# Score visits of four heads in one four-bank PSUM tile, and segment 0 cut into two query halves

## The chip, the core and the metric

The kernel runs on one core of a Trainium2 chip. A core has a matrix engine (PE, TensorE), a vector engine (DVE), an activation engine (ACT), a general engine (POOL, GpSimd), a sequencer that issues most DMAs (SP), an on-chip memory of 128 partitions (SBUF), and eight accumulation banks (PSUM) of 512 fp32 columns per partition, into which the matmuls of this kernel write. Each engine has a queue of its own instructions, in the order in which the program was compiled, and waits for others through semaphores. A matmul here is a weight load and a moving operand that is streamed past the weights; its moving columns are given in the text.

The metric is the device time of one execution in microseconds (us): the median of several runs.

## The reference

One transformer block on x of 2048 rows and 576 columns in bf16: attention with a compressive memory, then an FFN. Cut to what matters (32 heads of 18 columns, four segments of 512 rows; `phi(t)` is `t+1` above zero and `exp(t)` below):

```
h  = x + attention(layernorm(x)) @ wo
for s in range(4):                     # 512 rows each
    p     = softmax(qs @ ks.T * scale + causal mask)
    a_dot = p @ vs
    a_mem = (phi(qs) @ M) / (phi(qs) @ z + 1e-6)
    o     = g * a_mem + (1 - g) * a_dot          # g = sigmoid(beta), per head
    M, z  = M + phi(ks).T @ vs, z + sum(phi(ks))
h2 = h + gelu(layernorm(h) @ w1 + b1) @ w2 + b2  # inner width 4608
```

## The kernel before

**Phases.** The rows are 16 tiles of 128, four per segment. The program text calls `phase_P`, `phase_A`, `phase_B` for segments 0 to 3, and after them `phase_C` four times. Nobody writes the engines' orders by hand: a scheduler lays each engine's instructions in order by program order, priority and its own notion of when operands are ready. So the FFN's matmuls (phase C, last in the text) are put wherever PE would otherwise wait, and once compiled the order of each engine's queue is fixed. In what follows they are called filler.

- P (L218): per tile a layernorm (statistics on DVE, a power on POOL L182, scaling L183), five transposes (L195), a copy (ACT), 30 matmuls with 288 moving columns for Q, K and V (L203, L205), copies into padded layouts (ACT L72, DVE L268), 16 transposes (L259, L264) and their copies into `QT_al_s`, `KT_al_s` (DVE L260, L265). wq, wk and wv are loaded again for each segment through `load_w` (L102). At its end the memory matrix is updated (32 matmuls, L281).
- A (L300): eight groups of four heads. A group has three steps of key tiles: tile 0 (512 query columns), tiles 1 and 3 (384 and 128), tile 2 (256). In a step four heads' score matmuls use 32 rows of the PE array each (L338). They go into two tiles of two banks (`unit2`, L186; two buffers), two heads in each; each tile is followed by its own exponential (L347). POOL masks each diagonal block (L349), and PE multiplies the result with V (L356, 40 matmuls of 19 columns per group) into `ox`, which has one buffer. From segment 1 on each group has the memory part too: an exponential (L312), POOL L314, DVE L316, four matmuls (L323), normalising (L326 to L328). DVE ends the group at L361 to L371.
- B (L378): per tile five transposes, copy, ten matmuls with wo (all into one `unit2`), the residual add (L392), layernorm, five transposes, copy into `xn2T_s`. The two transpose results share a second `unit2`, one bank each.
- C (L405): per segment 36 blocks of FFN1 (five matmuls of 512 columns, L419 and L420, into one of three `psC` banks, DVE copy L424), a gelu after each twelve blocks (ACT L428, in place), and FFN2: per tile two chains of 36 matmuls of 288 columns (L437).

PSUM is split 2x2 banks (`psS`), 1 (`psX`), 3 (`psC`).

Of the kernel before, what the change touches and what calls it, by code (L numbers as in the profile page):

```python
# [8 lines left out]
ACT = mybir.ActivationFunctionType  # L9
# [7 lines left out]
def kernel(  # L17
# [15 lines left out]
    dbg = None  # L33
    nseg_run = None
# [15 lines left out]
    XW = 640  # L50
    scale = float(Dh) ** -0.5
    EPS = 1e-5
    BIG = 3.0e38
    GB = 3
    FORCE4 = False
    HIPRI = True
    GB = 3
    EVAC_ACT = 0
    XT_DVE = False
    QK_DVE = False  # L60

    def copy_xt(out, in_):
        if XT_DVE:
            nc.vector.tensor_copy(out=out, in_=in_)
        else:
            nc.scalar.copy(out=out, in_=in_)  # L66

    def copy_qk(out, in_):
        if QK_DVE:
            nc.vector.tensor_copy(out=out, in_=in_)  # L70
        else:
            nc.scalar.copy(out=out, in_=in_)  # L72
    if nseg_run is None:
        nseg_run = NSEG
# [3 lines left out]
    wpool = ctx.enter_context(tc.tile_pool(name="wpool", bufs=1))  # L78
# [5 lines left out]
    ptpool = ctx.enter_context(tc.tile_pool(name="ptpool", bufs=2))  # L84
    ptpool1 = ctx.enter_context(tc.tile_pool(name="ptpool1", bufs=1))
    hpool = ctx.enter_context(tc.tile_pool(name="hpool", bufs=2))
    hbpool = ctx.enter_context(tc.tile_pool(name="hbpool", bufs=1))
# [3 lines left out]
    psS = ctx.enter_context(tc.tile_pool(name="psS", bufs=2, space=PSUM))  # L91
    psX = ctx.enter_context(tc.tile_pool(name="psX", bufs=1, space=PSUM))
    psC = ctx.enter_context(tc.tile_pool(name="psC", bufs=3, space=PSUM))

    x_pre = []
    for tl in range(TPS):
        xt = xpool.tile([P, D], BF16, tag="x", name="xt") if tl < 2 else None
        if xt is not None:
            nc.sync.dma_start(out=xt[:], in_=x[tl * P:(tl + 1) * P, :])
        x_pre.append(xt)  # L100

    def load_w(W, tag):  # L102
        wt = wpool.tile([P, KT, D], BF16, tag=tag, name="wt_" + tag)
        nc.sync.dma_start(out=wt[:, 0:4, :], in_=W[0:512, :].rearrange("(k p) n -> p k n", p=P))
        nc.sync.dma_start(out=wt[0:64, 4, :], in_=W[512:576, :])
        nc.gpsimd.memset(wt[64:KTAIL, 4, :], 0.0)
        return wt

    w_pre = {"wq": load_w(A_wq, "wq"), "wk": load_w(A_wk, "wk"), "wvo": load_w(A_wv, "wvo")}
# [3 lines left out]
    maskcol = const.tile([P, 1], F32, name="maskcol")  # L113
    nc.vector.memset(maskcol[:], 0.0)
    for i in range(4):
        nc.vector.memset(maskcol[32 * i:32 * i + Dh, :], 1.0)
# [3 lines left out]
    beta_bc = const.tile([P, H], BF16, name="beta_bc")  # L120
    nc.sync.dma_start(out=beta_bc[:], in_=A_beta.partition_broadcast(P))
    g_bc = const.tile([P, H], F32, name="g_bc")
    nc.scalar.activation(out=g_bc[:], in_=beta_bc[:], func=ACT.Sigmoid)
    omg_bc = const.tile([P, H], F32, name="omg_bc")
    nc.vector.tensor_scalar(out=omg_bc[:], in0=g_bc[:], scalar1=-1.0, scalar2=1.0, op0=ALU.mult, op1=ALU.add)
    gmzm = const.tile([P, G, Dh], F32, name="gmzm")
    for i in range(4):
        src = g_bc[32 * i:32 * i + 32, :].rearrange("p (g i) -> p g i", i=4)[:, :, i:i + 1]
        nc.vector.tensor_scalar(out=gmzm[32 * i:32 * i + 32, :, :], in0=src.to_broadcast([32, G, Dh]),
                                scalar1=maskcol[32 * i:32 * i + 32, :], scalar2=None, op0=ALU.mult)  # L130

    b2_bc = const.tile([P, D], BF16, name="b2_bc")
    nc.sync.dma_start(out=b2_bc[:], in_=B_b2.partition_broadcast(P))
    b1_row = B_b1.rearrange("(o f) -> o f", o=1)
# [6 lines left out]
    q_pads = [const.tile([P, H, 32], BF16, name=f"q_pad{j}") for j in range(2)]  # L141
    k_pads = [const.tile([P, H, 32], BF16, name=f"k_pad{j}") for j in range(2)]
    phik_pads = [const.tile([P, H, 32], BF16, name=f"phik_pad{j}") for j in range(TPS)]
    v_augs = [const.tile([P, H, Dh + 1], BF16, name=f"v_aug{j}") for j in range(TPS)]
    xn_bufs = [const.tile([P, XW], BF16, name=f"xn{j}") for j in range(2)]
    xn2_bufs = [const.tile([P, XW], BF16, name=f"xn2_{j}") for j in range(1)]
    o_nat = const.tile([P, TPS, XW], BF16, name="o_nat")
    for tx in xn_bufs:
        nc.gpsimd.memset(tx[:, D:XW], 0.0)
    for tpad in q_pads + k_pads:  # L150
        nc.gpsimd.memset(tpad[:, :, Dh:32], 0.0)
    for tpad in phik_pads:
        nc.vector.memset(tpad[:, :, Dh:32], 0.0)
    for tv in v_augs:
        nc.vector.memset(tv[:, :, Dh:Dh + 1], 1.0)
    for tx in xn2_bufs:
        nc.gpsimd.memset(tx[:, D:XW], 0.0)
        nc.gpsimd.memset(tx[:, D:D + 1], 1.0)
    nc.gpsimd.memset(o_nat[:, :, D:XW], 0.0)

    hd = tc.dram_tile([S, D], F32, name="hd")
# [3 lines left out]
    late = {"x_last": None, "w2_last": None}  # L165

    def issue_w2():
        for c in range(4):
            d = nc.sync.dma_start(out=w2_sb[:, c * 9:(c + 1) * 9, :], in_=w2v[:, c * 9:(c + 1) * 9, :])
            if late["x_last"] is not None:  # L170
                tc.add_manual_dep(d.ins, late["x_last"].ins.name, SYNC_DEP, reason="bulk FFN weights after the first segment's inputs")
            late["w2_last"] = d
# [13 lines left out]
    def unit2():  # L186
        return psS.tile([P, 2, 512], F32, tag="st2", name="u2")

    def bf16v(bank_ap):
        return bank_ap.bitcast(BF16)  # L190

    def transposes5(src, bank_ap):
        pt = bf16v(bank_ap)[:, 0:KT * P].rearrange("p (k q) -> p k q", q=P)
        for k in range(KT):
            nc.tensor.transpose(out=pt[:, k, :], in_=src[:, k * P:(k + 1) * P], identity=ident[:])  # L195
        return pt

    def proj(xT_t, wt):
        u = unit2()
        for hf in range(2):  # L200
            ps = u[:, hf, :]
            for k in range(4):
                nc.tensor.matmul(out=ps[:, 0:HALF], lhsT=xT_t[:, k, :], rhs=wt[:, k, hf * HALF:(hf + 1) * HALF],  # L203
                                 start=(k == 0), stop=False)
            nc.tensor.matmul(out=ps[:, 0:HALF], lhsT=xT_t[0:KTAIL, 4, :], rhs=wt[0:KTAIL, 4, hf * HALF:(hf + 1) * HALF],  # L205
                             start=False, stop=True)
        return u

    def hview(u):
        return u[:, :, 0:HALF].rearrange("p b (h d) -> p b h d", d=Dh)  # L210

    def pad_view(tpad):
        return tpad[:, :, 0:Dh].rearrange("p (b h) d -> p b h d", b=2)

    st_P = {}
    st_B = {}

    def phase_P(s):  # L218
        if s == 0:
            wq_t, wk_t, wv_t = w_pre["wq"], w_pre["wk"], w_pre["wvo"]  # L220
        else:
            wq_t = load_w(A_wq, "wq")
            wk_t = load_w(A_wk, "wk")
            wv_t = load_w(A_wv, "wvo")
        QT_al_s = alpool.tile([P, G, L], BF16, tag="qt", name="QT_al_s")
        KT_al_s = alpool.tile([P, G, L], BF16, tag="kt", name="KT_al_s")
        for tl in range(TPS):
            t = s * TPS + tl
            cols = slice(tl * P, (tl + 1) * P)
            if s == 0 and x_pre[tl] is not None:  # L230
                xt = x_pre[tl]
            else:
                xt = xpool.tile([P, D], BF16, tag="x", name="xt")
                xd = nc.sync.dma_start(out=xt[:], in_=x[t * P:(t + 1) * P, :])
                if s == 0:
                    late["x_last"] = xd
                    if tl == TPS - 1:
                        issue_w2()
            xn = xn_bufs[tl % 2]
            layernorm(xt[:], xn)  # L240
            u0 = unit2()
            pt = transposes5(xn, u0[:, 0, :])
            xnT_t = xtp.tile([P, KT, P], BF16, tag="xnT", name="xnT_t")
            copy_xt(xnT_t[:], pt)
            uq = proj(xnT_t, wq_t)
            q_pad = q_pads[tl % 2]
            copy_qk(pad_view(q_pad), hview(uq))
            if dbg is not None and "q" in dbg:
                nc.sync.dma_start(out=dbg["q"][t * P:(t + 1) * P, :].rearrange("p (h d) -> p h d", d=Dh), in_=q_pad[:, :, 0:Dh])
            uk = proj(xnT_t, wk_t)  # L250
            k_pad = k_pads[tl % 2]
            copy_qk(pad_view(k_pad), hview(uk))
            ek = tmp1.tile([P, H, Dh], BF16, tag="e", name="ek")
            nc.scalar.activation(out=ek[:].rearrange("p (b h) d -> p b h d", b=2), in_=hview(uk), func=ACT.Exp)
            ut = unit2()
            ptq = bf16v(ut[:, 0, :]).rearrange("p (g q) -> p g q", q=P)
# [188 lines left out]
    if mode == "attn_first":  # L445
# [4 lines left out]
        for s in range(n):  # L450
            phase_C(s)
# [46 lines left out]
```

## Time and profile before

| what | value |
|---|---|
| three runs | 618.3, 619.83 (median), 621.29 us |
| span of the profiled execution | 618.1 us |
| mean granted PE clock | 0.939 |
| busy: PE, DVE, ACT, POOL | 553.5, 327.6, 319.4, 154.1 us |
| DMA | 54.65 MB, 88 GB/s in the mean |
| longest wait groups | POOL L401 for DVE L392 76.2 us; ACT L428 for DVE L424 55.7 us |

The page of a profile gives the busy time of each engine and, in 40 slices of 15.5 us, how busy each was and which clock PE was granted. A view by windows gives the same sums for chosen stretches: for each engine its busy time and, in brackets, its instructions. A view by time lists instructions: start, duration, engine, line, operation, output and inputs, sizes, count, and in square brackets the idle time before it with what ended it. A duration is not a price: FFN2's matmuls last 286 ns each by their rows, but 36 of them in a row take 4.41 us, 122.5 ns each. The distance from one start to the next is what a matmul costs PE. Idle time of an engine that sets nothing costs nothing.

### The profile page before, as it was taken

To read this page: it belongs to the slowest core of one execution; us is meant where nothing else is said; L and a number is where in the kernel's file an instruction comes from. 1 tells how busy PE (TensorE), PEld (TensorE's weight loads), DVE (VectorE), ACT (ScalarE), POOL (GpSimd) and SP (SyncE) were. 2 spreads that over 40 slices of the span, in tenths; PEclk is the share of its full clock that TensorE was granted. 3 is DMA by queue.
4 is the path that set the end of the run, shared out by engine and by line. 5 is a ranking of instruction groups with operands and counts; after the bars stand their busy time and mean duration, and the time that the engine had idled before them with its cause. 6 is when DMAs were issued, how large, how long until landed. Compare 5 with 4: busy or idle time off the path is not lost. (4 is left out here: it accounts for less than half of the span.)

```text
span 618.1 us, 12146 instructions
## 1 busy us (share of the span) xinstructions
PE 553.5 (90%) x4992; PEld 331.1 (54%) x4992; DVE 327.6 (53%) x811; ACT 319.4 (52%) x342; POOL 154.1 (25%) x247
## 2 busy tenths in 40 slices
PE   2778875599999998999999998899999999999997
PEld 1553333375444566675444466665544567744576
DVE  5443223467777635647786735555687641166310
ACT  1449951134999931338788742368767540024300
POOL 3124432313342223224323123135331210000000
PEclk9995555599999999999999999999999999999999
DMA  7960003325223113322132333111124432144020
GB/s 194 351 201 3 2 1 97 110 65 147 65 79 110 45 59 123 104 75 85 43 89 67 114 117 117 58 45 30 31 78 116 109 123 77 38 135 129 25 58 20
DMA packets 48223, 54.65 MB, mean 88 GB/s; under 512 B 3204, under 2 KB 44072, under 8 KB 48168
## 3 DMA queue, kind: packets, MB, share of 16 engines
q1 hardware_dynamic: 48168, 53.88, 29.3%
q8 instruction: 39, 0.64, 0.4%
q14 instruction: 16, 0.13, 0.1%
HBM read 46.79 MB, written 7.08 MB: 87 GB/s over the span
## 5 line engine op out<-in xcount | busy, mean ns | idle before, releaser
L437 PEld LDWEIGHTS <-hT 128*128 128x128 bf16 x1152 | 107.5, 98 | 30.3 <-issue 3.5
L428 ACT ACTIVATE hT<-hT 128x6144 bf16<-128x6144 bf16 x12 | 63.9, 5324 | 55.8 <-DVE hT L424 55.7
L419 PEld LDWEIGHTS <-w1g 128*128 128x128 bf16 x576 | 51.3, 98 | 56.0 <-issue 7.4
L203 PEld LDWEIGHTS <-xnT_t 128*128 128x128 bf16 x384 | 36.7, 100 | 24.3 <-ACT xnT_t L66 13.4
L338 PEld LDWEIGHTS <-KT_al_s 32*128 32x128 bf16 x512 | 21.0, 93 | 50.9 <-issue 47.9
L401 POOL TENSOR_TENSOR hb<-h_t,b_bc 128x576 f32<-128x576 f32 x16 | 20.4, 1277 | 76.2 <-DVE h_t L392 76.2
L182 POOL TENSOR_TENSOR rstd<-rstd,mhalf 128x1 f32<-128x1 f32 x32 | 17.5, 549 | 40.3 <-DVE rstd L181 40.3
L314 POOL TENSOR_SCALAR r_g<-QT_al_s 128x512 bf16<-128x512 bf16 x24 | 14.7, 612 | 36.1 <-DVE pq L316 33.4
L420 PEld LDWEIGHTS <-w1g 65*128 65x128 bf16 x144 | 14.0, 97 | 14.4 <-issue 0.6
L312 ACT ACTIVATE e_g<-QT_al_s 128x512 bf16<-128x512 bf16 x24 | 15.1, 630 | 11.4 <-DVE pq L316 8.0
L203 PEld LDWEIGHTS <-oT_t 128*128 128x128 bf16 x128 | 13.6, 109 | 11.0 <-issue 4.2
L316 DVE SCALAR_TENSOR_TENSOR pq<-e_g,r_g 128x512 bf16<-128x512 bf16 x24 | 19.2, 801 | 0.3
L195 PEld LDWEIGHTS <-xn_0_167 128*128 128x128 bf16 x80 | 5.2, 107 | 22.5 <-DVE xn_0_167 L183 21.6
L308 DVE MEMSET ox<- 128x456 f32 x32 | 14.0, 438 | 3.6 <-DVE o_nat L365 1.4
L177 DVE BATCH_NORM_STATS2 stats<-xt 128x6 f32<-128x288 bf16 x32 | 13.5, 441 | 3.9 <-DMA xt<-in_A_x_dram 3.8
L183 DVE TENSOR_SCALAR xn_0_167<-h_t,mv,rstd 128x576 bf16<-128x576 f32 x16 | 9.3, 579 | 9.9 <-POOL rstd L182 9.9
L323 PEld LDWEIGHTS <-pq 128*128 128x128 bf16 x96 | 8.1, 97 | 11.9 <-issue 5.6
L177 DVE BATCH_NORM_STATS2 stats<-h_t 128x6 f32<-128x288 f32 x32 | 13.1, 451 | 0.4
L270 POOL TENSOR_SCALAR rk<-k_pad_155 128x576 bf16<-128x576 bf16 x8 | 5.4, 678 | 28.0 <-ACT k_pad_155 L72 28.0
L205 PEld LDWEIGHTS <-xnT_t 65*128 65x128 bf16 x96 | 9.7, 101 | 2.8
L270 POOL TENSOR_SCALAR rk<-k_pad_156 128x576 bf16<-128x576 bf16 x8 | 5.3, 666 | 21.9 <-ACT k_pad_156 L72 21.2
L428 ACT ACT_TABLE_LOAD x8 | 10.3, 1283 | 0.1
(1911 smaller groups left out, 1416.8 us busy)
## 6 DMA issues: line engine op xcount, KB each, us to landing
w1g<-in_B_w_dram SPq DMA_DIRECT2D x36, 512.0 KB
w_sb<-in_B_w_dram SPq DMA_DIRECT2D x4, 1296.0 KB
hd<-hb SPq DMA_DIRECT2D x16, 288.0 KB
hc<-hd SPq DMA_DIRECT2D x16, 288.0 KB
xt<-in_A_x_dram SPq DMA_DIRECT2D x16, 144.0 KB
wt_wq<-in_A_wq_dram SPq DMA_DIRECT2D x4, 576.0 KB
wt_wk<-in_A_wk_dram SPq DMA_DIRECT2D x4, 576.0 KB
wt_wvo<-in_A_wv_dram SPq DMA_DIRECT2D x4, 576.0 KB
```

Of the source, the lines that this page charges most:

```text
L177: nc.vector.bn_stats(out=stats[:, c, :], in_=src[:, c * HALF:(c + 1) * HALF])
L182: nc.gpsimd.tensor_tensor(out=rstd[:], in0=rstd[:], in1=mhalf[:], op=ALU.pow)
L203: nc.tensor.matmul(out=ps[:, 0:HALF], lhsT=xT_t[:, k, :], rhs=wt[:, k, hf * HALF:(hf + 1) * HALF], start=(k == 0), stop=False)
L308: nc.vector.memset(ox[:, 0:456], 0.0)
L312: nc.scalar.activation(out=e_g[:], in_=QT_al_s[:, g, :], func=ACT.Exp)
L314: nc.gpsimd.tensor_scalar(out=r_g[:], in0=QT_al_s[:, g, :], scalar1=BIG, scalar2=0.0, op0=ALU.min, op1=ALU.max)
L316: nc.vector.scalar_tensor_tensor(out=pq[:], in0=e_g[:], scalar=1.0, in1=r_g[:], op0=ALU.min, op1=ALU.add)
L338: mm = nc.tensor.matmul(out=sts[i // 2][:, i % 2, off:off + n], lhsT=KT_al_s[rows, g, kt * P:(kt + 1) * P], rhs=QT_al_s[rows, g, kt * P:L] ...
L401: nc.gpsimd.tensor_tensor(out=hb[:], in0=h_t[:], in1=b2_bc[:], op=ALU.add)
L419: nc.tensor.matmul(out=ps[:], lhsT=w1g[:, k, j * P:(j + 1) * P], rhs=xn2T_s[:, k, :], start=(k == 0), stop=False)
L428: nc.scalar.activation(out=hT[:, f0:f1, :], in_=hT[:, f0:f1, :], func=ACT.Gelu_apprx_tanh)
L437: nc.tensor.matmul(out=ps[:, 0:HALF], lhsT=hT[:, f, tl * P:(tl + 1) * P], rhs=w2_sb[:, f, hf * HALF:(hf + 1) * HALF], start=(f == 0), stop ...
```

## The change

1. **Score visits.** PSUM is split 4 (`psS`, one buffer of four banks), 1 (`psX`), 2 (`psC`), 1 (`psB`). A "visit" puts the scores of four heads, one per bank, for up to 512 columns of (group, key tile) pairs into the one `banks4()` tile, followed by one exponential over all four banks. Written-out plans (`VISITS`) pack pairs of neighbouring groups into full visits: 20 per segment.
2. **One bank for the rest.** Transposes, the wo product (in two halves), the memory product and the memory update each take the single `bank()` (`psB`). FFN banks go from three to two.
3. **Projection.** wq, wk and wv lie side by side in a resident tile, loaded once; Q, K and V of a tile are four chains of five matmuls with 432 columns. wo is resident too. The mask on `KT_al_s` is dropped.
4. **Segment 0 in halves.** P, A and B run for tiles 0 and 1, and then for tiles 2 and 3; the FFN of each half is a unit of its own, whose FFN1 matmuls have 256 moving columns. w1 is so streamed five times and not four.
5. **Memory part.** All four query tiles in one product, with no clearing of the output between them.
6. **Start.** beta is loaded on POOL's queue, wk on ACT's; the gate is computed with an exponential and a reciprocal, after the first two tiles' projection. w2 comes in six DMAs after the inputs of segment 0's second half.

```diff
-    psS = ctx.enter_context(tc.tile_pool(name="psS", bufs=2, space=PSUM))
+    psS = ctx.enter_context(tc.tile_pool(name="psS", bufs=1, space=PSUM))
     psX = ctx.enter_context(tc.tile_pool(name="psX", bufs=1, space=PSUM))
-    psC = ctx.enter_context(tc.tile_pool(name="psC", bufs=3, space=PSUM))
+    psC = ctx.enter_context(tc.tile_pool(name="psC", bufs=2, space=PSUM))
+    psB = ctx.enter_context(tc.tile_pool(name="psB", bufs=1, space=PSUM))
+    def bank():
+        return psB.tile([P, 512], F32, tag="b", name="bk")
+    def banks4():
+        return psS.tile([P, 4, 512], F32, tag="st4", name="st4")
...
+            u = banks4()
+            for c in range(4):
+                mm5(u[:, c, 0:CH], lambda r, k: xnT_t[r, k, :], lambda r, k: wqkv[r, k, c * CH:(c + 1) * CH])
...
+            nc.scalar.copy(out=qk[:, 0:24, 0:Dh], in_=uh[0])
+            nc.scalar.copy(out=qk[:, 24:48, 0:Dh], in_=uh[1])
+            nc.vector.tensor_copy(out=qk[:, 48:64, 0:Dh], in_=uh[2][:, 0:16, :])
+            nc.vector.tensor_copy(out=v_aug[:, 0:8, 0:Dh], in_=uh[2][:, 16:24, :])
+            nc.vector.tensor_copy(out=v_aug[:, 8:32, 0:Dh], in_=uh[3])
+            for dst, g0 in ((QT_al_s, 0), (KT_al_s, G)):
+                ptq = bf16v(bank()[:]).rearrange("p (g q) -> p g q", q=P)
+                for g in range(G):
+                    tr = nc.tensor.transpose(out=ptq[:, g, :], in_=qk2d[:, (g0 + g) * P:(g0 + g + 1) * P], identity=ident[:])
+                nc.vector.tensor_copy(out=dst[:, :, cols], in_=ptq)
...
+    VISITS = {
+        (0, 4): (2, [[(0, 0)], [(0, 1), (0, 3)], [(0, 2), (1, 2)], [(1, 0)], [(1, 1), (1, 3)]]),
+        (0, 2): (4, [[(0, 0), (0, 1), (1, 1)], [(1, 0), (2, 0)], [(2, 1), (3, 0), (3, 1)]]),
+        (2, 4): (4, [[(0, 0), (0, 1)], [(0, 2), (0, 3), (1, 3)], [(1, 0), (1, 1)], [(1, 2), (2, 0)],
+                     [(2, 1), (2, 2)], [(2, 3), (3, 3), (3, 0)], [(3, 1), (3, 2)]]),
+    }
...
-            for si, step in enumerate(steps):
-                sts = [unit2(), unit2()]
...
-                for hp in range(2):
-                    prev_exp = nc.scalar.activation(out=pt_[:, 2 * hp:2 * hp + 2, :], in_=sts[hp][:, :, 0:W], func=ACT.Exp, scale=scale)
+        for visit in visits:
+            st = banks4()
+            with tc.high_priority():
+                for g, kt in visit:
+                    lo = max(kt, qa)
+                    n = (qb - lo) * P
+                    for i in range(4):
+                        last_visit[s] = nc.tensor.matmul(out=st[:, i, off:off + n], lhsT=KT_al_s[rows, g, kt * P:(kt + 1) * P],
+                                         rhs=QT_al_s[rows, g, lo * P:qb * P], start=True, stop=True,
+                                         tile_position=(32 * i, 0))
+            pt_ = ptpool.tile([P, 4, 512], BF16, tag="pt", name="pt")
+            nc.scalar.activation(out=pt_[:, :, 0:off], in_=st[:, :, 0:off], func=ACT.Exp, scale=scale)
...
-            uo = proj(oT_t, wo_t)
+            for hf in range(2):
+                hs = slice(hf * HALF, (hf + 1) * HALF)
+                ps = bank()[:, 0:HALF]
+                mm5(ps, lambda r, k: oT_t[r, k, :], lambda r, k: wo_t[r, k, hs])
+                nc.vector.tensor_tensor(out=h_t[:, hs], in0=ps, in1=xt2[:, hs], op=ALU.add)
...
-    for s in range(n):
-        phase_P(s)
-        phase_A(s)
-        phase_B(s)
-    for s in range(n):
-        phase_C(s)
+    phase_P(0, lo)
+    gates()
+    load_wo()
+    phase_A(0, 0, 2)
+    phase_B(0, lo)
+    phase_P(0, hi)
+    load_w2()
+    phase_A(0, 2, 4)
+    phase_M(0)
+    phase_B(0, hi)
+    for s in range(1, NSEG):
+        phase_P(s, whole)
+        if s < NSEG - 1:
+            phase_M(s)
+        phase_A(s, 0, 4)
+        phase_B(s, whole)
+    phase_C(0, lo)
+    phase_C(0, hi)
+    for s in range(1, NSEG):
+        phase_C(s, whole)
```

Where each phase stands in PE's compiled queue of the changed kernel, with the filler between its first and last matmul ("F1h" are FFN1 matmuls of 256 columns, "F1" of 512, "F2" those of FFN2):

| stage (segment, tiles) | filler in it |
|---|---|
| P, A, B of segment 0, tiles 0 and 1 | none |
| P, A, B of segment 0, tiles 2 and 3 | 40 F1h; 140 F1h and 114 F2; 30 F2 |
| P, A, B of segment 1 | 130 F1h; 50 F1h and 144 F2, all ahead of the last five visits; none |
| P, A, B of segment 2 | 85 F1; 95 F1 and 177 F2; 111 F2 |
| P, A, B of segment 3 | 85 F1; 95 F1 and 190 F2; 98 F2 |
| rest | 180 F1, 288 F2 |

## The prediction

> **What bounds the kernel now.** I read three views: the page's slices, the windows cut at the phases' borders, and the timeline inside one phase of each kind. The slices first:
>
> ```profile
> PE   2778875599999998999999998899999999999997
> ACT  1449951134999931338788742368767540024300
> PEclk9995555599999999999999999999999999999999
> ```
>
> From the ninth slice on PE is busy to the end: filler closes its gaps. Ahead of that, in segment 0, no filler exists, and for five slices PE even ran at half clock. The windows say the same in microseconds (PE, weight loads, DVE, ACT, POOL, clock, DMA):
>
> ```profile
> 0.00:43.00 43.00, 23.72 (x207) 18.01 (x208) 20.55 (x58) 12.88 (x19) 11.03 (x29) 1.00 0.82 246
> 43.00:88.20 45.20, 36.58 (x480) 17.75 (x479) 13.45 (x41) 40.10 (x48) 19.54 (x32) 0.55 0.08 23
> 88.20:119.30 31.10, 15.64 (x78) 9.33 (x79) 11.68 (x30) 5.29 (x8) 8.33 (x10) 0.50 0.31 95
> 150.90:223.20 72.30, 71.56 (x740) 35.55 (x739) 49.92 (x143) 65.80 (x63) 23.75 (x38) 1.00 0.27 78
> 223.20:249.20 26.00, 22.55 (x192) 16.49 (x190) 12.76 (x34) 5.54 (x8) 8.38 (x10) 1.00 0.40 123
> ```
>
> These are P, A, B of segment 0 (119.3 us), then A and B of segment 1. So the bound is PE's work plus what PE loses where filler is missing or doesn't fit. I therefore split each stage's time into filler (FFN1 of 512 columns starts every 0.217 us, five in 1.08; FFN2 of 288 every 0.1225) and the rest, its **own time**. Filler is 720 x 0.217 + 1152 x 0.1225 = 298 us wherever it stands; counting it by window leaves:
>
> | own time, us | seg 0 | seg 1 | seg 2 | seg 3 |
> |---|---|---|---|---|
> | P | 43.0 | 23.4 | 22.9 | 22.9 |
> | A | 45.2 | 30.6 | 31.7 | 30.5 |
> | B | 31.1 | 11.9 | 11.4 | 9.9 |
>
> and 5.1 after the last B: 319.6 in all, 618.1 with the filler.
>
> **The change, part by part.** The same split on the changed queue order (the filler table above).
>
> *Score visits.* Before, in A of segment 1:
>
> ```profile
> 161.70 0.39 PE L419 MATMUL ps_f_5513<-xn2T_s,w1g 128*128 128x512 bf16 x1
> 162.03 0.39 PE L338 MATMUL u_1970<-QT_al_s,KT_al_s 32*128 32x512 bf16 x2
> 162.34 0.39 PE L419 MATMUL ps_f_5513<-xn2T_s,w1g 128*128 128x512 bf16 x1
> 162.67 0.39 PE L338 MATMUL u_1971<-QT_al_s,KT_al_s 32*128 32x512 bf16 x2
> ```
>
> A pair of heads holds PE for 0.31 us, and the FFN matmul ahead of it costs 0.33, not 0.22: 0.41 per pair of 512 columns, 0.30 per pair of 256. A group has four of the first kind and two of the second: 2.24 us. Four heads at once cost PE what two do if they stream together (the heads of the unfilled part do: both pairs are in flight there), so a visit costs 0.41, 2.5 per group: 1.03. That saves 1.2 us per group.
> Exponentials: 1.02 us for 1024 elements and 0.60 for 512 give 0.83 ns per element and, for 2048, 1.87 (bounds: 1.70 without a fixed part, 2.04 twice the 1024).
>
> What it adds is a loop: one tile of four banks means that the next scores wait for the whole exponential. At full clock that is 0.43 (scores to exponential) + 1.87 + 0.05 = 2.35 us per visit, 2.57 at half clock (0.65). The masks come next:
>
> ```profile
> 53.75 1.22 POOL L349 TENSOR_SCALAR_AFFINE_SELECT pt_671<-pt_671 128x512 bf16<-128x512 bf16 x2 [1.44 <-ACT pt_671 L347]
> ```
>
> In the new order the V products of a visit stand right behind the scores of the next. Scores run 0.05 to 0.37 after the exponential's end, the first mask is ready at 0.74 and a second at 1.37; PE waits in between with the filler queued behind. Two groups: five visits 2.05, 80 V products at 0.026 = 2.05, memory 0.4, mask waits 1.2 (nothing, if PE is late anyway; 2.5, if every second mask is waited out): 5.7, or 2.85 per group against about 3.7 before. A of segment 2: 8 x 2.85 + 1.4 (memory update) + 1.0 (end) + 1.4 (two gelus of 5.32 us and two table loads each, which the 36 to 60 FFN matmuls put there nearly cover) = **26.6**; of segment 3 **25.2**.
>
> *One bank for B.* Before, one tile:
>
> ```profile
> 229.65 0.69 ACT L66 COPY xn2T_s<-u_2571 128x640 bf16<-128x640 bf16 x1 [1.86 <-PE u_2571 L195]
> 231.82 0.76 DVE L392 TENSOR_TENSOR h_t<-u_2620,xt_2631 128x576 f32<-128x576 f32 x1 [2.35 <-PE u_2620 L205]
> 232.63 0.44 PE L195 MATMUL u_2653<-ident,o_nat 128*128 128x128 bf16 x5
> 235.18 0.45 PE L195 MATMUL u_2612<-ident,xn_0_167 128*128 128x128 bf16 x5 [0.76 <-DVE xn_0_167 L183]
> ```
>
> The next tile's transposes (232.63) run under the layernorm of this one; period 6.0 us. With one bank they can't, and the two wo halves wait for each other's add. Chain: first half to its add 0.81, add 0.45, second half 0.86, add 0.45; second statistics, aggregate, power and scaling 2.2; transposes and copy 1.2; the next tile's transposes and copy 1.2: 7.2 us. At half clock (wo to add 2.60 us in B of segment 0 against 1.42 here) 8.9. Four tiles with filler: 30 less 13.6 of filler = **16.4** in segment 2, 29.5 - 12.0 = **17.5** in 3.
>
> *Filler gone from B of segment 1.* The halves let FFN work start early, but it is used up five visits ahead of the end of A(1), and the next comes only with the layernormed rows of B(1). Five visits x 2.5 + 3.2 (masks, V products, end of a group) + four tiles x 8.9 + 0.9 is 52 us with nothing to fill. Own time of A(1): 15 visits x 1.14 + 1.4 + 3.4 (gelu, end) + 15.7 = **37.6**; of B(1) **36.5**. If the clock stays up there: 28.9 for the tiles. Here a row and a rule differ:
>
> ```profile
> 62.00:77.00 15.00, 12.91 (x166) 6.08 (x168) 3.50 (x10) 14.43 (x19) 7.33 (x12) 0.50 0.01 2
> ```
>
> PE stood idle for 2.1 of 15 us in all and still had half clock. The Trainium skill ("TensorE: Matmul & The Clock Gate", "HAM oscillation — how this bites in real kernels") asks only for no PE gap over about 3.4 us. By it B(1) would keep its clock and the sum fall by some 6 us; I take the row.
>
> *Projection, one bank and two FFN banks in P.* A filled tile: 21 transposes at 0.056, 20 matmuls at 0.183 (scaled from 0.1225 for 288 columns): 4.84 us, as before. DVE's queue then holds K copy 0.42, V copies 0.85, Q copy 0.69, phi 0.76, FFN copy 0.69, K transposes' copy 0.69 in this order; the third FFN bank waits behind these, and so does the next tile's transpose. I charge 1.1 us of waits (0 if the queue fits, 2.5 if each copy is late): 5.9 per tile. Own time: P(2) 23.6 + 1.7 (it starts at half clock, 3.4 us of work) = **25.3**, P(3) **24.1**, P(1) **25.4** (a gelu stands ahead of the fourth tile's copies).
>
> *Weights resident.* Three reloads of 2.6 MB go. Hidden before (DMA share 0.29 in P), worth nothing.
>
> *Segment 0.* First projection at 7.0 us (before 12.73, when ACT sat 9.79 us for beta); 5.6 (half clock first) + 3.1 (Q, K through one bank) + 1.3 + 3.7 + 3.9 to the first exponential: 24.6. Six visits: 5 x 2.6 + 1.87 + masks 1.9, V and end of group 1.8: **18.6**. B, two tiles at 8.9: **18.0**. Filler now starts at 61.2 and not at 119.8. Then P 13.6 own, A (14 visits x 1.1 + 1.4 + gelus 3 + a late w1 group behind w2's 5.3 MB, 1) **20.8**, B 15 - 3.7 = **11.3**. FFN1 of 256 columns isn't in the trace: 0.108 (half) to 0.1225 (288 columns); I take 0.109, range +5 us.
>
> **Sum**, own time: segment 0 106.9 (before 119.3), 1: 99.5 (65.9), 2: 68.3 (66.0), 3: 66.8 (63.3), end 5.6 (5.1): 347.1. Filler 297.4. Span 644.5, 26.4 over the span of before; the runs' median lies 1.7 over it, so **646 us**.
>
> **Rivals.**
> - *Visits carry it* (not slower). The masks and gelus cost PE nothing, and A pays for its PE work alone, 8 x 2.25 + 1.4 = 19.5 instead of 26.6. That takes 7.1 from A(2) and A(3) each, 5 from A(1) and A(0): 24.5, 621 us. For it: ACT has slack, and POOL is a quarter busy. Against: the products stand directly behind the scores. It decides from an own time of 2.3 us per group down; with any further gain the kernel is faster.
> - *The clock stays up in segment 1.* Four tiles at 7.2, five visits at 2.35, P(2) at full speed: 9.6 less, 636. Against: the row above.
> - *Two FFN banks are too few.* DVE's in-order copies hold PE in P and A: 2.2 us on each of seven half-segments' A and P, 15 more: 661. For it: DVE needs about 8 of 10 us in a P tile.
> - *Four heads don't stream together*, so the change doesn't do what it says: 80 visits (6, 14 and three times 20) of 0.2 more, 662.
>
> **How the numbers follow.** Forecast 0.5 (634 to 656), clock 0.15, banks 0.14, no streaming 0.03, visits 0.18. Its own bounds (exponential, masks, P waits, 256 columns) reach about 12 either way. Range 621 to 664, which leaves out about 0.13 below and 0.07 above. Within 0.5% (3.1 us) a measurement can't tell it from no change. Visits: faster 0.07, same 0.07, slower 0.04; of the other cases 0.04 faster by errors that I can't name. Faster 0.11, same 0.08, slower 0.81.
>
> **What would show it.** The windows of the changed kernel: filler (FFN lines) from about 61 us; a stretch of about 50 us near 230 to 285 without FFN lines, PE clock 0.5; a period of 7 to 9 us from one L368 pair to the next; masks (L338) named as what V products wait for; P tiles about 10 us apart. Wrong would be: FFN work inside B(1), or A(2) under 62 us.

## The result, and the profile after

| | before | changed |
|---|---|---|
| median of the runs | 619.61 us | 682.41 us (678.15 to 684.54) |
| ratio to before, 95% interval | 1 | 1.100 (1.096 to 1.104) |
| span of the profiled execution | 618.1 us | 682.8 us |
| mean granted PE clock | 0.939 | 0.883 |

The kernel is 10% slower; 646 us was forecast, with a range up to 664. Below, kernels are compared by their ratio to the kernel before, which ran beside each of them. Some executions of the kernels that use two tiles of two banks (e3, e5, e8), and one of e6, ran at a lower clock: the ratios leave these out, the medians don't.

The slices of the changed kernel (17.1 us each: busy tenths, and the granted clock):

```profile
PE   3644768895998884449998999869989999679998
ACT  1261137851257875111296985112588963113500
PEclk9755789997999995558999999979999999879999
```

PE is full from the ninth slice on before; here it has two large holes. The first is the start. The second is in slices 16 to 18, where the clock falls to a half. Smaller ones lie in slices 10 and 27 and near 590 us. The windows of A and B of segments 1 and 2, and B of segment 3 (PE, weight loads, DVE, ACT, POOL, clock, DMA share and GB/s):

```profile
206.40:271.50 65.10, 49.22 (x717) 33.91 (x716) 33.70 (x94) 48.50 (x32) 24.93 (x40) 0.84 0.15 46
271.50:307.30 35.80, 16.30 (x78) 8.67 (x79) 13.76 (x35) 5.54 (x8) 7.94 (x9) 0.50 0.15 50
350.30:423.90 73.60, 66.36 (x795) 39.55 (x795) 42.05 (x104) 57.61 (x35) 25.31 (x40) 0.98 0.20 62
423.90:456.30 32.40, 24.52 (x193) 16.65 (x192) 16.55 (x43) 5.54 (x8) 7.96 (x9) 0.89 0.23 74
569.50:603.00 33.50, 23.56 (x180) 15.96 (x179) 13.29 (x35) 5.56 (x9) 7.29 (x8) 0.84 0.19 62
```

B of segment 1 has 78 matmuls where the kernel before had 192: no FFN work is left for it, as forecast. It takes 35.8 us (before 26.0 with 14.1 us of FFN work in it).

What PE waited for in the whole span, in us, times and the longest:

```profile
PE bk L187 <- DVE xn__136 L181: 32.1, 16, 2.7
PE ox L348 <- POOL pt L338: 14.6, 32, 1.7
PE bk L187 <- DVE xn L181: 13.9, 5, 10.7
PE ox L348 <- DVE ox L301: 10.4, 9, 1.8
PE st L329 <- ACT pt L335: 8.7, 9, 2.0
```

In order: layernorms in B with nothing beside them, the masks, the start, the clearing of the single `ox` behind the group ahead, and the exponentials. The waits inside A (masks, `ox`, exponentials) hardly existed before (masks and `ox` together some 6 us).

The same split into filler (FFN work at its price, 297.5 us) and own time shows where the forecast held:

| stage | before | forecast | measured | | stage | before | forecast | measured |
|---|---|---|---|---|---|---|---|---|
| P(0) first half | | 24.6 | **32.8** | | B(1) | 11.9 | 36.5 | 35.8 |
| A(0) first half | | 18.6 | **23.4** | | P(2) | 22.9 | 25.3 | 24.6 |
| B(0) first half | | 18.0 | 17.7 | | A(2) | 31.7 | 26.6 | **31.3** |
| P(0) second half | | 13.6 | 14.7 | | B(2) | 11.4 | 16.4 | 18.8 |
| A(0) second half | | 20.8 | **27.3** | | P(3) | 22.9 | 24.1 | 23.5 |
| B(0) second half | | 11.3 | 13.1 | | A(3) | 30.5 | 25.2 | 27.4 |
| P(1) | 23.4 | 25.4 | 25.9 | | B(3) | 9.9 | 17.5 | **21.5** |
| A(1) | 30.6 | 37.6 | **42.1** | | end | 5.1 | 5.6 | 5.5 |

The sum is 385.3 against 347.1. Of the 38 us, 13 lie in the first half's P and A, 18 in the other phases A and 8 in the filled phases B; the rest gives 1 back. Of the 18, over 4 have nothing to do with scores. In A of segment 0's second half PE waited for the first w1 groups, whose transfers were issued behind those of w2 (that window's waits):

```profile
PE fbk L192 <- DMA w1g<-in_B_w_dram: 5.3, 3, 3.3
```

### The profile page after: what moved, and what is told of

It is laid out like the page before. It is cut to its first block, busy times and chain, and to the rows that moved or that the text cites. A ratio compares the mean times of both kernels' runs of the same rounds, so it can differ in the third digit from the quotient of the medians.

```text
span 682.8 us, 12117 instructions
## 1 busy us (share of the span) xinstructions
PE 547.2 (80%) x5076; PEld 334.5 (49%) x5076; DVE 329.9 (48%) x797; ACT 314.3 (46%) x236; POOL 149.2 (22%) x232
## 4 chain that ended last, share of the span: by engine, by line
PE 40%; ACT 18%; issue 16%; DVE 14%; POOL 7%; DMA 4%; SPq 0%; ACTq 0%; POOLq 0%
PE fbk L192 10%; PE fbk L407 10%; ACT pt L335 9%; PE st L192 6%; ACT hT L397 5%; POOL pt L338 4%; DMA w1g<-in_B_w_dram 4%; PE st L329 2%; PE fbk L193 2%; PE ox L348 2%; DVE hT L394 2%; PE bk L187 2%; POOL rstd L180 1%; PE st L193 1%; POOL h_t L372 1%
## 5 line engine op out<-in xcount | busy, mean ns | idle before, releaser
L192 PE MATMUL fbk<-xn2T_s,w1g 128*128 128x512 bf16 (+1 forms) x720 | 167.4, 350 | 13.7 <-DVE hT L394 7.0
L335 ACT ACTIVATE pt<-st 128x2048 bf16<-128x2048 f32 x80 | 150.1, 1877 | 59.5 <-PE st L329 53.4
L407 PE MATMUL fbk<-w_sb,hT 128*128 128x288 bf16 x1152 | 153.5, 286 | 0.6 <-ACT hT L397 0.6
L394 DVE CAST hT<-fbk 128x512 bf16<-128x512 f32 x144 | 98.5, 685 | 77.4 <-PE fbk L193 77.3
L338 POOL TENSOR_SCALAR_AFFINE_SELECT pt<-pt 128x512 bf16<-128x512 bf16 x128 | 80.2, 646 | 149.2 <-ACT pt L335 149.2
L397 ACT ACTIVATE hT<-hT 128x6144 bf16<-128x6144 bf16 (+1 forms) x13 | 64.1, 4929 | 29.7 <-DVE hT L394 29.6
L348 PE MATMUL ox<-v_aug,pt 128*128 128x19 bf16 x1280 | 51.8, 174 | 28.2 <-POOL pt L338 14.6
L348 PEld LDWEIGHTS <-pt 128*128 128x128 bf16 x1280 | 41.5, 97 | 52.7 <-POOL pt L338 38.7
L192 PE MATMUL st<-wqkv,xnT_t 128*128 128x432 bf16 x256 | 64.3, 378 | 1.9 <-ACT xnT_t L212 1.9
L193 PE MATMUL fbk<-xn2T_s,w1g 65*128 65x512 bf16 (+1 forms) x180 | 62.3, 347 | 0.2 <-DMA w1g<-in_B_w_dram 0.2
L409 DVE TENSOR_TENSOR ot<-fbk,hc 128x288 bf16<-128x288 f32 x32 | 14.6, 455 | 64.4 <-PE fbk L407 64.4
L368 DVE TENSOR_TENSOR h_t<-bk,xt 128x288 f32<-128x288 f32 x32 | 14.7, 458 | 59.0 <-PE bk L193 59.0
L192 PEld LDWEIGHTS <-xnT_t 128*128 128x128 bf16 x256 | 26.2, 106 | 30.6 <-issue 8.2
```

What stands on the lines that cost most here:

```text
L192: nc.tensor.matmul(out=ps, lhsT=lhsT_of(slice(0, P), k), rhs=rhs_of(slice(0, P), k), start=(k == 0), stop=False)
L193: nc.tensor.matmul(out=ps, lhsT=lhsT_of(slice(0, KTAIL), 4), rhs=rhs_of(slice(0, KTAIL), 4), start=False, stop=True)
L335: nc.scalar.activation(out=pt_[:, :, 0:off], in_=st[:, :, 0:off], func=ACT.Exp, scale=scale)
L338: nc.gpsimd.affine_select(out=pt_[:, :, o:o + P], in_=pt_[:, :, o:o + P], pattern=[[0, 4], [1, P]], compare_op=ALU.is_ge, fill=0.0, base=0 ...
L348: nc.tensor.matmul(out=o_ps[:, qt - qa, i, :], lhsT=pt_[:, i, blk:blk + P], rhs=v_augs[kt][:, 4 * g + i, :], start=False, stop=False, skip ...
L368: nc.vector.tensor_tensor(out=h_t[:, hs], in0=ps, in1=xt2[:, hs], op=ALU.add)
```

## The experiments

Thirteen kernels ran. The theory after the result: the new work is done as forecast, but A with its one four-bank tile costs more than it saves, and the start was priced too low. Rivals were the halves of segment 0, the single bank of B, and the two FFN banks.

**e1: segment 0 whole again.**

```diff
-    phase_A(0, 0, 2)
-    phase_B(0, lo)
     phase_P(0, hi)
     load_w2()
-    phase_A(0, 2, 4)
     phase_M(0)
-    phase_B(0, hi)
+    phase_A(0, 0, 4)
+    phase_B(0, whole)
...
-    phase_C(0, lo)
-    phase_C(0, hi)
-    for s in range(1, NSEG):
+    for s in range(NSEG):
```

> The changed kernel with segment 0 whole again (20 visits over all four query tiles, one FFN unit of 512 columns); all else kept. Theory (filler is a fixed amount, 298 us, and starting it earlier only moves the place where it is missing): no FFN matmul until about 152 us (projection 57, visits 59, B four tiles at 9.0), then the hole in B of segment 1 is gone and segments 1 and 2 take 149 each, segment 3 147, the last FFN 80: span about 676, 6 less than the changed kernel (from 18 less to 6 more). Rival 1 (the early start is a real gain of some 45 us): 30 to 45 us longer. Rival 2 (the hole in segment 1 is the loss, halving alone made the kernel slower): 35 to 48 us shorter.

Measured: 679.12 us, ratio 1.095 (1.090 to 1.099); span 675.5. Four windows of it: P, A and B of segment 0, B of segment 1.

```profile
0.00:58.00 58.00, 31.14 (x160) 15.72 (x160) 21.33 (x67) 10.78 (x18) 10.54 (x24) 0.82 0.58 176
58.00:115.50 57.50, 28.66 (x492) 17.31 (x492) 13.73 (x43) 37.54 (x20) 19.87 (x32) 0.52 0.01 1
115.50:151.20 35.70, 16.27 (x77) 8.65 (x77) 13.71 (x35) 5.54 (x8) 7.93 (x9) 0.50 0.15 50
269.00:299.70 30.70, 22.84 (x175) 15.32 (x173) 14.99 (x39) 5.54 (x8) 7.95 (x9) 0.87 0.24 77
```

The last row has 175 matmuls: the hole of segment 1 is filled, and segment 0 is without filler until 151.2 instead of 73.9 us. One is paid with the other. So the halves are neither the gain nor the loss of this kernel; they move the place where filler is missing.

**e2: no masks. e9: masks kept, V products two visits later.**

```diff
-            for g, kt, lo, o in placed:
-                if kt >= qa:
-                    nc.gpsimd.affine_select(out=pt_[:, :, o:o + P], in_=pt_[:, :, o:o + P],
...
```

```diff
+            pend.append((pt_, placed))
+            if len(pend) == 3:
+                products(*pend.pop(0), last_visit[s])
```

In e9 the first product of a visit is ordered behind the scores of the visit after the next.

> The changed kernel without the masks on POOL (L338), so attention is not causal inside the diagonal blocks; no other work changes. Theory (the V products stand right behind the next scores and wait for the mask): the waits of V products for POOL in the trace, 14.6 us in all phases A, go, and little comes in their place: 10 to 16 us less than the changed kernel; own time of A(2) from 31 to about 28. Rival (the loop over the one four-bank tile, scores to exponential and back, holds A, and the mask only fills that time): 0 to 3 us less.

> The changed kernel, masks and one four-bank tile kept, with the V products of a visit placed behind the scores of the visit after the next, so that the masks are done before PE comes to them. Theory (what the masks cost is PE standing in front of them, as e2 showed without them): waits for POOL L338 gone, 657 to 664. Rival (the delay moves the wait to the exponential or to the single ox tile): 674 to 683.

Measured: e2 659.15 us, ratio 1.063 (1.058 to 1.068), 23 us less than the changed kernel and more than was expected. e9 672.31 us, ratio 1.081 (1.078 to 1.084), 10 less: between theory and rival. PE's waits in e9:

```profile
PE st L350 <- ACT pt L356: 15.1, 13, 2.0
PE ox L330 <- DVE ox L301: 8.3, 7, 2.0
```

The waits for masks shrink from 14.6 to 1.1 us, but those for the exponential grow from 8.7 to 15.1. Half of what the masks cost comes back as the next wait of the same loop. Why e2 gained 23 and not 15 isn't settled: it also leaves out POOL's work and gives the scheduler another order (A(0)'s second half alone falls by 5.9 in own time, where the wait for w1 is 2.5 us and no longer 5.3).

**e3: each four-bank tile as two tiles of two banks.**

```diff
-    psS = ctx.enter_context(tc.tile_pool(name="psS", bufs=1, space=PSUM))
+    psS = ctx.enter_context(tc.tile_pool(name="psS", bufs=2, space=PSUM))
...
-        return psS.tile([P, 4, 512], F32, tag="st4", name="st4")
+        return [psS.tile([P, 2, 512], F32, tag="st2", name="st2") for _ in range(2)]
...
-            nc.scalar.activation(out=pt_[:, :, 0:off], in_=st[:, :, 0:off], func=ACT.Exp, scale=scale)
+            for hp in range(2):
+                nc.scalar.activation(out=pt_[:, 2 * hp:2 * hp + 2, 0:off], in_=st[hp][:, :, 0:off], func=ACT.Exp, scale=scale)
```

> The changed kernel with each four-bank tile as two tiles of two banks (two buffers), two heads and one exponential in each; the visits, the halves, the single bank and two FFN banks stay. Theory (four heads at once save PE 1.2 us a group where it is full; one tile costs a loop where it is not): A(2) and A(3) 4 to 10 us longer each in own time, the unfilled stretches about 0.5 us a visit shorter (26 visits): span about 690 (680 to 702). Rival (the single four-bank tile is what makes A slow): A(2) falls from 31 to 26 to 28, span 660 to 670.

Measured: 638.74 us, ratio 1.019 (1.013 to 1.026). The theory fell, and the rival's time was too timid: undoing this one part takes back eight of the ten per cent (seven by the medians). The rival's other sign, an own time of 26 to 28 us in A(2), did not come: in e8, which keeps the pairs, it is some 36. The visits, the halves, the single bank of B and the two FFN banks are all still there.

**e4: wo and the second transposes of B in the four-bank tile.**

```diff
+            u = banks4()
...
-                ps = bank()[:, 0:HALF]
+                ps = u[:, hf, 0:HALF]
...
-            pt2 = transposes5(xn2)
+            pt2 = transposes5(xn2, u[:, 2, :])
```

> The changed kernel with the wo product and the second transposes of B in the four-bank tile, which is idle in B; the first transposes keep the single bank. Theory (the single bank serialises B: 9.0 us per tile without filler, 7.5 with it): 7.0 and 5.9 us per tile, with 2 + 2 + 4 + 8 tiles some 20 to 28 us less than the changed kernel, span 655 to 663. Rival (B is held by its own chain of add, statistics, power, scaling and copies, whatever bank it uses): 0 to 6 us less.

Measured: 663.46 us, ratio 1.070 (1.064 to 1.075), 19 less. B of segment 1, still without filler, and B of segment 2:

```profile
266.10:297.20 31.10, 15.89 (x77) 9.01 (x77) 13.69 (x35) 5.54 (x8) 7.94 (x9) 0.50 0.18 57
415.40:441.80 26.40, 20.89 (x176) 14.91 (x174) 14.69 (x39) 5.54 (x8) 7.95 (x9) 1.00 0.28 91
```

A tile takes 7.8 us instead of 9.0 in the one and 6.6 instead of 7.6 in the other: the single bank did serialise B, for a little less than was charged.

**e5: e3 with segment 0 whole.** The edits of e3 and e1 together.

> The kernel of e3 (two tiles of two banks; 631 and 634 in its undisturbed executions) with segment 0 whole instead of in halves. Theory (an early start of the FFN pays only as long as its supply is not used up before the next unit comes; with pairs it is not, so here the halves are worth their 15 to 25 us): 648 to 657. Rival (the halves give nothing by themselves, as e1 showed on the changed kernel): 626 to 636.

Measured: a median of 662.65 us, and no ratio; the one execution that is left took 643.45 us, against 630.93 and 634.17 of e3. By that one number the halves are worth some 10 us here, below the theory's range and above the rival's. It isn't more than a hint.

**e6: the kernel before with two FFN banks. e13: the same, with the free bank as a second buffer of `ox` (`psX`, bufs=2).**

```diff
-    psC = ctx.enter_context(tc.tile_pool(name="psC", bufs=3, space=PSUM))
+    psC = ctx.enter_context(tc.tile_pool(name="psC", bufs=2, space=PSUM))
```

> The kernel before with two FFN banks instead of three, nothing else changed (one bank stays unused). Theory (two banks cost little, since a block's copy takes 0.69 us of the 1.08 that the next block takes on PE): 0 to 4 us more than before. Rival (DVE's copies hold PE where there are only two banks): some 15 us more.

> The kernel before with two FFN banks, as in e6, and the bank that this frees as a second buffer of ox. Theory (waits for ox, 3.6 us in the kernel before, go; two FFN banks are enough): 613 to 617 where the kernel before has 620. Rival (the waits for ox lie beside FFN work): 617 to 620, as e6.

Measured: e6 618.77 us, ratio 0.996 (0.994 to 0.997); e13 618.46 us, ratio 0.996 (0.994 to 0.999). Taking the third FFN bank away cost the kernel before nothing, it gained 0.4%. A second `ox` adds nothing to that. So the rival of the two FFN banks has no support; in the changed kernel PE did wait for their copies, 7.0 us in all, and that is under half of what the rival asked for. These two are the only versions that beat both kernels, by about as much as can be told.

**e7 and e10: the kernel before with beta loaded early; in e10 with the gate's work behind the first copy and scalings.**

```diff
+    nc.gpsimd.dma_start(out=beta_bc[:], in_=A_beta.partition_broadcast(P))
-    nc.sync.dma_start(out=beta_bc[:], in_=A_beta.partition_broadcast(P))
...
+        tc.add_manual_dep(o1.ins, after[0].ins.name, ORDER, reason="gate behind the first layernorms")
+        tc.add_manual_dep(a1.ins, after[1].ins.name, ORDER, reason="gate behind the first copy")
```

> The kernel before with beta loaded at the start on POOL's queue, nothing else changed. Theory (ACT waits 9.79 us for beta and the first copy of transposes behind it): first projection matmul at about 8 us instead of 12.73, 3 to 5 us less in all: 615 to 617. Rival (the first projection then waits for the weights instead): 0 to 1 us less.

> The kernel before with beta loaded at the start on POOL's queue, as in e7, and with the gate's activation behind the first copy on ACT and its DVE work behind the first two scalings. Theory (in e7 the gate's DVE work, put ahead of the layernorm in the queue, took the place of ACT's wait: the scaling came at 11.65 us instead of 5.75): first projection matmul at 7.5 to 9.5 us, 615 to 618. Rival (the weights land only at about 12 us): 619 to 622.

Measured: e7 622.62 us, ratio 1.002 (1.000 to 1.004); e10 623.2 us, ratio 1.003 (1.001 to 1.004). Neither gained. In e7, DVE's queue by time:

```profile
7.71 1.18 DVE L130 TENSOR_SCALAR gmzm<-g_bc,maskcol 32x144 f32<-32x144 f32 x4
9.29 1.18 DVE L178 BATCH_NORM_STATS2 stats<-xt 128x6 f32<-128x288 bf16 x3
11.65 0.42 DVE L184 TENSOR_SCALAR xn<-xt,mv,rstd 128x576 bf16<-128x576 bf16 x1
```

The gate, now early in the order, stands ahead of the layernorm and waits for beta, so the scaling comes at 11.65 instead of 5.75. In e10 the first projection does start at 9.07, and then:

```profile
14.22 1.18 DVE L182 BATCH_NORM_STATS2 stats<-xt 128x6 f32<-128x288 bf16 x3 [6.18 <-DMA xt<-in_A_x_dram]
18.27 0.68 DVE L267 COPY QT_al_s<-u 128x1024 bf16<-128x1024 bf16 x1
19.00 1.01 PE L271 MATMUL u<-ident,k_pad 128*128 128x128 bf16 x8 [4.33 <-POOL rstd L187]
```

DVE waits 6.18 us for the rows of the third tile, and Q's copy, which has been ready since about 14.7, stands behind it. The wait was moved twice and never removed.

**e8: e3 with B's banks as before, and the gate behind the layernorms. e11: the changed kernel with e9, e4 and the same gate.** Both repair the score loop, B and the gate; they differ in the tile, in e9's delay and in the banks that B uses. Of e8's edit only the gate is shown:

```diff
+        tc.add_manual_dep(g1.ins, late["ln"].ins.name, ORDER, reason="gate behind the first layernorms")
```

> The kernel of e3 with B's transposes in one tile of two banks and its wo halves in the other, as the kernel before has them, and the gate's work on DVE behind the first two layernorms' scaling. Theory (with FFN work in B the single bank costs less than 1 us per tile, without it 2; the gate 3 us at the start): 620 to 627. Rival (B's own chain and the weights' landing decide): 630 to 634.

> The changed kernel with three repairs: late V products as in e9, wo and second transposes in the four-bank tile as in e4, the gate behind the first layernorms. Theory (the losses lie one after another and add): 682 less some 20, 20 and 3: 633 to 645. Rival (the hole in segment 1 takes up what the others free): 650 to 662.

Measured: e8 626.86 us, ratio 1.005 (1.002 to 1.009). e11 651.67 us, ratio 1.046 (1.042 to 1.050): 31 us less than the changed kernel, about the sum of what e9 (10), e4 (19) and the gate (P(0)'s first half 29.4 instead of 32.8) gave. The number lies in the rival's range; but the parts do add, and the expectation was wrong because it had put e9 at 20. What ACT's exponentials waited for, by the score tile's list of idle times, first in e8 and then in e11:

```profile
  PE st L330: 15.9, 30
```

```profile
  PE st L351: 32.7, 45
```

Over the whole traces PE stood idle for 115 us in e11 and for 60 in e8 (136 in the changed kernel, 65 before). A's own time does not show this gain. A of segment 2, in e8 and in e11:

```profile
289.90:345.10 55.20, 52.56 (x614) 24.85 (x614) 39.31 (x103) 49.09 (x51) 26.32 (x40) 0.91 0.16 44
331.70:406.40 74.70, 69.03 (x811) 41.56 (x817) 43.21 (x109) 57.70 (x35) 24.77 (x40) 0.95 0.21 61
```

It is 20 us shorter in e8, but has less filler in it (87 FFN1 matmuls; in e11 89, and 198 of FFN2). Own time is some 36 us in e8 and 31 in e11, PE's idle time 2.6 and 5.7. With two tiles A asks for less filler, and what it doesn't take is left for the phases behind it. How much of the 29 us between the two traces comes this way, and how much from B's banks or from the projection, which uses the split tile too, isn't shown.

**e12: e11 with 144 FFN2 matmuls kept for B of segment 1.**

```diff
+                    if f == 0 and s == 0 and tls[0] == 2:
+                        tc.add_manual_dep(m2.ins, last_visit[1].ins.name, ORDER, reason="kept for B of segment 1")
```

> The kernel of e11 with the FFN2 matmuls of segment 0's second half (144, 17.6 us) held back until the scores of segment 1 are done; nothing else changed. Theory (it is the place of the filler: between visits of A it lengthens A, which runs at the pace of the exponentials, and is then missing in B): A of segment 1 from 63 to 50 to 56 us, B of segment 1 from 31 to 26 to 29 with FFN work in it, clock 0.9 or more there: 652 less 8 to 18, 634 to 644. Rival (the supply alone counts, and the hole only moves into A): 648 to 654.

Measured: 648.16 us, ratio 1.045 (1.041 to 1.048): the rival's number. Windows in A and B of segment 1, and what PE waited for in A:

```profile
220.00:235.00 15.00, 6.33 (x124) 4.06 (x127) 7.09 (x23) 11.66 (x8) 6.12 (x11) 0.50 0.00 1
262.00:285.00 23.00, 20.06 (x169) 14.60 (x168) 12.83 (x36) 4.15 (x6) 6.77 (x9) 1.00 0.25 84
```

```profile
PE st L351 <- ACT pt L357: 24.3, 15, 6.2
```

B did what the theory said: 26.1 us at full clock. A did not: 65.2 us with 8.8 us of FFN work in it, where e11 took 63.2 with 23.1 and e8 53.4 with 15.7. So A(1) with one tile takes some 63 to 65 us whether it is filled or not, and the filler's place decided only which phase shows the hole. The two aren't quite alike, since the unfilled part ran at half clock. The wait of 6.2 us is one in which a gelu of 4.04 us, a table load of 1.28 and an exponential stand between PE and its tile.

That loop, in the unfilled end of A(1) of the changed kernel, on ACT and on PE:

```profile
255.83 1.88 ACT L335 ACTIVATE pt<-st 128x2048 bf16<-128x2048 f32 x1 [0.80 <-POOL pt L338]
258.48 1.88 ACT L335 ACTIVATE pt<-st 128x2048 bf16<-128x2048 f32 x1 [0.78 <-PE st L329]
```

```profile
255.08 0.61 PE L329 MATMUL st<-QT_al_s,KT_al_s 32*128 32x512 bf16 x4 [1.03 <-ACT pt L335]
257.75 0.62 PE L329 MATMUL st<-QT_al_s,KT_al_s 32*128 32x384 bf16 x8 [1.10 <-ACT pt L335]
```

Scores can start only when the whole tile has been read (257.71), and the exponential only when all four heads are there (258.48): each engine waits for the other once per visit, 2.65 us from one to the next, of which 1.88 is work of ACT. (For the first exponential the view names POOL; its scores had ended at 255.69, 0.14 us ahead of it.) Two tiles let ACT read one while PE fills the other. What that is worth by itself shows in A of segment 0 where it is whole and has no filler: 45.2 us in the kernel before, 57.5 with one four-bank tile (e1's second window), and with the same visits in two tiles (e5):

```profile
53.80:98.20 44.40, 35.85 (x491) 18.25 (x490) 14.88 (x43) 38.16 (x40) 19.90 (x32) 0.58 0.01 2
```

ACT's work is the same (37.5 and 38.2 us); the one tile costs 13 us.

## Why the prediction went wrong

The sign held, and so did most steps. The size did not: 38 us more of own time than the sum had. Two steps failed, the score visits and the start, and two terms were too small, the late w1 group and B.

- **Filler gone from B(1): right.** B(1) measured 35.8 for 36.5, P(2) 24.6 for 25.3. The rival that kept the clock up falls: the clock was 0.50 through all of B(1).
- **One bank for B: right, a little low.** A tile took 9.0 us without filler (8.9 forecast) and about 7.5 with it (7.2). B(3) measured 21.5 instead of 17.5, since its filler ended at 589 us, before the layernorms of its last two tiles, which the forecast had as filled. e4 prices the bank at 19 us.
- **P, FFN banks, the end: right** within 1.1 us per stage, but for the first half of P(0). The two FFN banks cost the kernel before nothing (e6).
- **Four heads stream together: right.** Score matmuls with what they add to an FFN matmul ahead of them take 13.0 us in A(2), mask waits behind them included; before 18.2.
- **Segment 0's start: the step that failed first.** "First projection at 7.0 us" was 12.16: the gate's work, which the text puts after two tiles, was placed ahead of the first scaling on DVE, from 7.59 to 10.13 us:

```profile
8.49 1.64 DVE L148 TENSOR_SCALAR gmzm<-g_bc,maskcol 32x144 f32<-32x144 f32 x4
10.17 0.77 DVE L181 TENSOR_SCALAR xn<-xt,mv,rstd 128x576 bf16<-128x576 bf16 x2
12.16 1.62 PE L192 MATMUL st<-wqkv,xnT_t 128*128 128x432 bf16 x4 [0.79 <-ACT xnT_t L212]
```

Putting it behind gave 3.4 us in e11, and nothing in the kernel before, where another wait followed. In e11 the projection started at 9.67, after PE had waited 1.35 us for wq's landing, so the weights too kept it from 7.0. The second tile's projection, charged 3.7 us at full clock, ran nearly to its end at a half, from 23.16 to 30.0. With A of this half (23.4 for 18.6; PE waited 4.5 us there for the clearing of `ox`) that is 13 us of the 38.
- **The late w1 group: a term that was too small.** "A late w1 group behind w2's 5.3 MB, 1" was 5.3 us of waiting, and A(0)'s second half 27.3 instead of 20.8.
- **Score visits: the step that failed worst.** "The next scores wait for the whole exponential" stood there with its period of 2.35 us (2.65 measured at half clock), and was then used only where there is no filler. Where there is, A was priced by PE's work with mask waits of 1.2 us per two groups: 26.6 for A(2), measured 31.3, as much as before (31.7). A(2) in the kernel before, to lay beside the window of 350.30 above:

```profile
278.80:352.80 74.00, 71.93 (x720) 33.58 (x719) 54.86 (x147) 58.60 (x60) 23.41 (x38) 1.00 0.28 80
```

Without the filler (42.3 us in both) PE was busy for 24.1 us and before for 29.6: of the credited 8 x 1.2 us, 5.5 came. But PE stood idle for 7.2 us and before for 2.1, which takes them back. The masks, which the sum had at 4.8 in A(2), are 2.9 of that; a wait of 1.7 for an FFN bank's copy and 1.4 for `ox` aren't in the sum at all. In A(1) the largest waits are the exponentials' (6.4) and the masks' (5.6). A saving of PE's work was credited as time of A where PE had begun to wait for the other engines.
- **What this hid.** The forecast blamed the 34 us that it added to segment 1 on the halves. e1 shows that without them much the same time is lost in segment 0. With two tiles, the halves kept, B of segment 1 has FFN work and full clock again (e8):

```profile
227.70:255.80 28.10, 24.26 (x208) 18.38 (x209) 15.98 (x40) 8.68 (x8) 7.96 (x9) 1.00 0.44 133
```

The four-bank tile carries 8 of the 10 per cent (e3), 4 of them even after the other repairs (e8 against e11, with B's banks). The sum was near for B(1), and the reason given for it was only the occasion.
- **The rivals.** "Visits carry it" has no support: no whole A came near 19.5. "Two FFN banks" (661) and "four heads don't stream together" (662) were nearest by number, 20 us short, and not by cause.

## What to carry to other kernels

When a tile becomes so large that only one fits, write down the loop between its producer and its consumer and compare it with the elapsed time of the phase also where other work fills the gaps: a saving on one engine is nothing if the two now take turns. Work that fills gaps is a fixed amount: starting it earlier only moves the place where it runs out, unless the critical chain gets shorter. And on an in-order queue the removal of one wait is worth only what separates it from the next one: look at what stands behind it before crediting it.

## What the runs showed of the hardware

The clock. In the changed kernel it fell to a half at about 255 us, where the longest pause of PE in the 20 us ahead was 1.0 us. In e8 it stayed at a half for 30 us although PE's records, whose ends are modelled, leave no pause:

```profile
85.00:100.00 15.00, 15.00 (x183) 7.34 (x183) 6.12 (x23) 11.78 (x13) 4.33 (x8) 0.50 0.03 10
100.00:115.00 15.00, 15.00 (x158) 7.32 (x158) 4.30 (x15) 10.59 (x11) 4.06 (x7) 0.50 0.29 80
```

That stretch is A of segment 0's second half: scores on 32 rows, V products of 19 columns, FFN1 of 256 columns. A PE that is busy by its records was thus not enough for a full clock there. The rule weighed in the prediction, no gap over about 3.4 us (the Trainium skill, "TensorE: Matmul & The Clock Gate", "HAM oscillation — how this bites in real kernels"), was kept in both cases, and the clock was a half all the same. What the clock does follow wasn't tried.

The exponential of 2048 elements took 1.877 us, as scaled from the two smaller sizes (1.87).
